# Two small projection matrices moved to the front of two hardware DMA queues

## The chip, the cores and the metric

One core of one Trainium2 chip runs the whole program. The metric is the device time of one execution in microseconds (us). A run's profile gives, besides that time, a span from the first to the last instruction, some 2 us shorter. One run of the kernel before (124.2 us) that was slow is left out of the ratios. The sets of runs were made on different chips, so times are compared as ratios to the kernel before, run in the same set.

## The reference, cut to what matters

A linear attention with a sketched feature map, followed by a feed-forward network (FFN) with a ReLU gate. Inputs q, k, v have shape 4 x 4 x 1088 x 32; S1 and S2 are only 8 x 32.

```python
def phi(x):
    a = np.einsum('rd,bhsd->bhsr', S1, x)
    b = np.einsum('rd,bhsd->bhsr', S2, x)
    return np.einsum('bhsi,bhsj->bhsij', a, b).reshape(*x.shape[:-1], r * r)
q_p, k_p = (phi(q), phi(k))
kv = np.einsum('bhsf,bhsd->bhfd', k_p, v)
z = np.sum(k_p, axis=2)
# num = q_p kv, den = q_p z, x = num / den, then per token:
# (relu(x @ w_gate) * (x @ w_val)) @ w_out
```

Nothing can be projected before both S1 and S2 are on the chip.

## The kernel before: the parts that matter

The loads of the first batch are issued at the start from three engines: SP (SyncE) and ACT (ScalarE), which have a hardware queue each, and GpSimd (POOL), which has a software queue. In the profile SP's queue is q1, ACT's q10 and GpSimd's q0.

```python
xall = const.tile([128, 2, D], FP32, name="xall")
for sm, i in ((S1, 0), (S2, 1)):                      # ACT: S1, then S2, 16 KB each on the chip
    nc.scalar.dma_start(out=xall[:, i], in_=sm[None].to_broadcast([16, R, D]))
for i in range(2):
    load_k0(i, nc.sync)                               # SP: the two halves of k, 272 KB each
load_kq(q4, q, 0)                                     # SP: q, 544 KB
# ... cut: masks on GpSimd ...
for g in range(4):
    load_v(0, g)                                      # GpSimd: v in four pieces
for i in range(2):
    load_w(i)                                         # GpSimd: FFN weights
# ... cut: GpSimd builds mkv and an identity, then load_w(2) ...
```

Then comes the chain that this study is about. It is part of the head, the stretch before the first FFN matmul:

- VectorE (DVE) transposes each half of k (`kT`).
- It turns S into `y`, `s1f` and `s_bd`.
- TensorE (PE) projects k with `s_bd` (line 209).
- DVE moves the result to `kab`, transposes q (`qT`), and with GpSimd forms the outer products `kp`.

A small scheduler in Python, run when the program is built, fixes each engine's order from assumed landing times (`LAND`). Each engine's instructions then ran in that order, waiting where a load was late.

## Time and profile before

| | before |
|---|---|
| median (first three runs) | 123.22 us |
| span of the profiled run | 121.5 us |
| first FFN matmul | 24.03 us |
| from there to the end of the span | 97.5 us |

The page divides the span into 40 slices of 3.04 us; a digit is the busy share in tenths. From the page of the kernel before:

```profile
PE   5008996999999998999999999999999999999940
...
DVE  2215999747999998889584769858774799899940
...
DMA  3899945199926030002002000300300120201003
```

PE reads 0 in slices 2 and 3, while the DMA engines read 8 and 9. The DVE timeline of the kernel before says what it waited for (start, duration, line, operation; the bracket gives the idle time ahead and what ended it):

```profile
3.62 0.74 DVE L197 STREAM_TRANSPOSE kT<-k 128x544 f32<-128x544 f32 x1 [1.81 <-DMA k<-in_k_dram]
8.58 0.24 DVE L177 STREAM_TRANSPOSE y<-xall 128x64 f32<-128x64 f32 x1 [4.21 <-DMA xall<-in_S_dram]
...
9.01 0.74 DVE L197 STREAM_TRANSPOSE kT<-k 128x544 f32<-128x544 f32 x1
11.07 0.85 DVE L216 STREAM_TRANSPOSE kab<-ps_a 128x288 f32<-128x288 f32 x2 [1.32 <-PE ps_a L209]
```

The 4.21 us ahead of `y` are the wait for S.

### The profile page before, as it was taken

Reading aid. Unit: us, or ns where it says so; the run is one execution under the profiler, and the core shown is the slowest. Engines: PE = TensorE matmul, PEld = TensorE weight load, DVE = VectorE, ACT = ScalarE, POOL = GpSimd, SP = SyncE. Lnnn points to the kernel's source line nnn. Section 1 sums busy time; section 2 is a strip of 40 time slices with the busy share of each in tenths; the row PEclk is TensorE's granted clock in tenths of the full one; section 3 lists DMA queues with packets and bytes.
Section 4 is the critical chain, followed back from the end, with each engine's and each line's share of the span. In section 5 each row is a group of like instructions: output and inputs, shape, how many; then the busy total and the mean of one; then the engine's idle time right before and its main releaser. Section 6 shows DMA issues by size and latency. Waiting matters only on the chain.

```text
span 121.5 us, 3061 instructions
## 1 busy us (share of the span) xinstructions
PE 106.6 (88%) x1149; PEld 63.8 (52%) x1149; DVE 90.0 (74%) x184; ACT 81.5 (67%) x160; POOL 63.4 (52%) x84
## 2 busy tenths in 40 slices
PE   5008996999999998999999999999999999999940
PEld 4003673534555765445676646666555666766620
DVE  2215999747999998889584769858774799899940
ACT  3100003377368989778799997879998977987730
POOL 7930816984979997329999232797653000000000
PEclk9999999999999999999999999999999999999996
DMA  3899945199926030002002000300300120201003
GB/s 92 242 220 199 109 145 222 4 298 261 360 26 70 5 86 3 5 11 75 0 5 70 16 0 5 86 0 5 89 0 3 42 50 0 64 22 32 17 0 86
DMA packets 7662, 9.20 MB, mean 76 GB/s; under 512 B 2912, under 2 KB 5216, under 8 KB 7648
## 3 DMA queue, kind: packets, MB, share of 16 engines
q1 hardware_dynamic: 3120, 6.56, 16.8%
q0 software_dynamic: 4144, 2.29, 14.4%
q10 hardware_dynamic: 384, 0.16, 0.7%
q8 instruction: 9, 0.15, 0.5%
q14 instruction: 5, 0.04, 0.1%
HBM read 9.08 MB, written 2.23 MB: 93 GB/s over the span
## 4 chain that ended last, share of the span: by engine, by line
PE 67%; DVE 9%; POOL 9%; DMA 6%; ACT 4%; issue 1%; DVEq 1%; ACTq 1%
PE v_ps L594 18%; PE g_ps L583 17%; PE ot_ps L407 16%; DMA xall<-in_S_dram 6%; PE ps_a L209 4%; PE ps_a L366 4%; POOL qp L234 3%; PE ps_a L389 2%; ACT g_sb L588 2%; DVE kp L234 2%; POOL kp L234 2%; PE ps_a L316 2%; DVE ht L611 1%; POOL v L104 1%; PE kv_ps L250 1%
## 5 line engine op out<-in xcount | busy, mean ns | idle before, releaser
L611 DVE TENSOR_TENSOR ht<-g_sb,v_ps 128x512 f16<-128x512 f16 (+1 forms) x98 | 60.6, 647 | 14.4 <-ACT g_sb L588 6.2
L588 ACT ACTIVATE g_sb<-g_ps 128x512 f16<-128x512 f32 (+1 forms) x108 | 59.4, 585 | 13.3 <-PE g_ps L583 10.6
L594 PE MATMUL v_ps<-xT,wv_sb 128*128 128x512 f16 (+1 forms) x108 | 40.2, 372 | 0.0
L407 PE MATMUL ot_ps<-wo_sb,ht 128*128 128x128 f16 x408 | 39.1, 219 | 0.4 <-DVE ht L611 0.4
L407 PEld LDWEIGHTS <-ht 128*128 128x128 f16 x408 | 30.2, 98 | 16.4 <-issue 1.4
L583 PE MATMUL g_ps<-xT,wg_sb 128*128 128x512 f16 (+1 forms) x108 | 38.0, 377 | 0.8 <-ACT g_sb L588 0.7
L234 POOL TENSOR_TENSOR kp<-kab 128x512 f16<-128x512 f32 (+2 forms) x16 | 16.6, 1057 | 7.3 <-DVE kab L216 7.3
L234 POOL TENSOR_TENSOR qp<-a,qab 128x512 f16<-128x512 f32 (+2 forms) x17 | 17.5, 1049 | 0.3
L605 POOL TENSOR_TENSOR ht<-g_sb,v_sb 128x512 f16<-128x512 f16 x10 | 11.6, 1163 | 8.7 <-ACT v_sb L600 8.7
L594 PEld LDWEIGHTS <-wv_sb 128*128 128x128 f16 x108 | 10.6, 98 | 5.6 <-issue 3.7
L366 PE MATMUL ps_a<-ident,qp 128*128 128x128 f16 (+1 forms) x72 | 10.3, 235 | 1.1 <-ACT qptx L374 0.6
L583 PEld LDWEIGHTS <-wg_sb 128*128 128x128 f16 x108 | 10.0, 100 | 1.4 <-issue 0.7
L374 ACT COPY qptx<-ps_a 128x1024 f16<-128x1024 f16 (+1 forms) x10 | 8.9, 892 | 2.2 <-PE ps_a L366 2.2
L366 PEld LDWEIGHTS <-qp 128*128 128x128 f16 (+1 forms) x72 | 6.4, 104 | 7.0 <-issue 2.2
L209 PE MATMUL ps_a<-kT,s_bd 64*32 64x288 f32 x64 | 4.3, 482 | 6.4 <-DVE s_bd L179 6.4
L104 POOL DMA_DIRECT2D v<-in_v_dram x16 | 8.9, 564 | 0.1
L680 PE MATMUL ot_ps<-zeros 128*128 128x128 f16 x45 | 7.9, 308 | 1.1 <-DVE zeros L151 1.1
L250 PEld LDWEIGHTS <-kp 128*128 128x128 f16 (+1 forms) x72 | 5.9, 106 | 4.6 <-issue 3.2
L250 PE MATMUL kv_ps<-v,kp 128*128 128x64 f16 (+1 forms) x72 | 8.1, 207 | 0.0
L334 POOL TENSOR_TENSOR bw<-qab,qw 128x256 f32<-128x256 f32 (+2 forms) x5 | 3.1, 626 | 8.2 <-DVE qw L325 8.2
L197 DVE STREAM_TRANSPOSE kT<-k 128x544 f32<-128x544 f32 x8 | 5.7, 723 | 1.8 <-DMA k<-in_k_dram 1.8
L270 ACT COPY zs<-kv_ps 128x32 f32<-128x32 f32 x4 | 0.7, 182 | 9.1 <-PE kv_ps L264 9.1
(68 smaller groups left out, 84.4 us busy)
## 6 DMA issues: line engine op xcount, KB each, us to landing
q<-in_q_dram SPq DMA_DIRECT2D x4, 544.0 KB, 6.4
out_dram<-o_sb SPq DMA_DIRECT2D x30, 64.0 KB, 1.7
k<-in_k_dram SPq DMA_DIRECT2D x3, 544.0 KB, 4.2
v<-in_v_dram POOLq DMA_DIRECT2D x8, 72.0 KB, 5.2
k<-in_k_dram SPq DMA_DIRECT2D x2, 272.0 KB, 3.0
v<-in_v_dram POOLq DMA_DIRECT2D x8, 64.0 KB, 5.6
wg_sb<-in_moe_w_gate_dram POOLq DMA_DIRECT2D x1, 384.0 KB, 7.4
wv_sb<-in_moe_w_val_dram POOLq DMA_DIRECT2D x1, 384.0 KB, 8.7
```

The costliest lines, as they stand in the source:

```text
L104: nc.gpsimd.dma_start(out=v4[b][32 * g:32 * g + 32, :, 0:n].rearrange("p h c d -> p h (c d)"), in_=x[:, :, CB[g] * D:(CB[g] + n) * D],)
L209: nc.tensor.matmul(st["ps", key][rp][32 * g:32 * g + 32, lo:lo + 32 * n], s_bd[64 * rp:64 * rp + 64].rearrange("p h r x -> p (h r x)"), xt ...
L234: eng.tensor_tensor(out=dst, in0=a[:, :, :, None].to_broadcast([np, n, R, R]), in1=bb[:, :, None, :].to_broadcast([np, n, R, R]), op=ALU.mult)
L250: nc.tensor.matmul(ps[:, p].rearrange("p (h d) -> p h d", h=2), st["kp", b, c][0:np, p * 128:(p + 1) * 128], v4[b][0:np, 2 * p:2 * p + 2, ...
L366: nc.tensor.transpose(st["qpt", key, p0][:, p, c * n:(c + 1) * n], st["qp", key, p0][0:n, c, p * 128:(p + 1) * 128], ident16[0:n, 0:n])
L374: nc.scalar.copy(out=t[:, :, c0 * n:c1 * n], in_=st["qpt", key, p0][:, :, c0 * n:c1 * n])
L407: nc.tensor.matmul(st["ot", i][:, t], st["ht", i][:, j, t * 128:(t + 1) * 128], wo_sb[:, j], start=(j == 0 and t == 0), stop=True, skip_gr ...
L583: nc.tensor.matmul(st["g", n][:, :cs], wg_sb[:, j], xT[:, c0:c0 + cs], start=True, stop=True)
L588: nc.scalar.activation(out=st["gs", n][:, :cs], in_=st["g", n][:, :cs], func=ACTF.Relu)
L594: nc.tensor.matmul(st["v", n][:, :cs], wv_sb[:, j], xT[:, c0:c0 + cs], start=True, stop=True)
L605: nc.gpsimd.tensor_tensor(out=st["ht", i][:, j, :cs], in0=st["gs", n][:, :cs], in1=st["vs", n][:, :cs], op=ALU.mult)
L611: nc.vector.tensor_tensor(out=st["ht", i][:, j, :cs], in0=st["gs", n][:, :cs], in1=st["v", n][:, :cs], op=ALU.mult)
```

## The change

The intent is to give S1 and S2 a hardware queue's first place each, so that both land early, and to let k follow.

```diff
-LAND = {"s": 4.2, "k": (3.9, 4.9), "q": 6.9, "v": 8.2, "w": (10.8, 13.2, 15.8)}
+LAND = {"s": 3.4, "k": (4.0, 5.0), "q": 7.0, "v": 8.2, "w": (10.8, 13.2, 15.8)}
@@
-    for sm, i in ((S1, 0), (S2, 1)):
-        nc.scalar.dma_start(out=xall[:, i], in_=sm[None].to_broadcast([16, R, D]))
+    for sm, i, eng in ((S1, 0, nc.sync), (S2, 1, nc.scalar)):
+        eng.dma_start(out=xall[:, i], in_=sm[None].to_broadcast([16, R, D]))
     for i in range(2):
         load_k0(i, nc.sync)
     load_kq(q4, q, 0)
```

The new `LAND` moves `y`, `s1f` and `s_bd` ahead of the first k transpose on DVE. PE's and GpSimd's orders stay as they were.

## The prediction

> **What bounds the kernel now.** I began with the page's digits per slice. From about 25 us to 117 us TensorE (PE) reads 9 in nearly every slice, so that stretch is full of work that the change does not touch. Slices 2 and 3 (3 to 9 us) read 0 for PE, nearly 0 for VectorE (DVE): the head of the kernel waits for data. The last releasing chain says for what. This is its start, in order of time (start, duration, what):
>
> ```profile
> 0.81 0.64 ACTq L111
> 1.45 0.03 issue
> 1.48 7.00 DMA xall<-in_S_dram
> ...
> 8.58 0.24 DVE y L177
> 8.82 0.17 DVE s1f L185
> 9.00 0.11 DVE s_bd L179
> ...
> 9.15 1.94 PE ps_a L209 x16
> 11.09 0.83 DVE kab L216 x2
> ```
>
> The reader is to see that the second of two 16 KB transfers, S2, is the longest piece of the head: issued at 1.48, landed at 8.48. Everything up to there hangs on it. I then asked for the transfers of that tile, for time from issue to landing:
>
> ```profile
> DMA to landing us min/median/max: 3.0/5.0/7.0
> ```
>
> Two transfers, so S1 took 3.0 us (0.81 to 3.8) and S2 took 7.0, though both are equal in size and came from the same queue 0.64 us apart. The packets that left on that queue (q10) in the stretches 3:4, 4:5, 5:6, 6:7 and 7:8 us tell why (packets, MB, share of 16 engines):
>
> ```profile
> q10 hardware_dynamic: 118, 0.01, 9.7%
> ...
> q10 hardware_dynamic: 63, 0.01, 8.1%
> ...
> q10 hardware_dynamic: 40, 0.00, 3.3%
> ...
> q10 hardware_dynamic: 25, 0.00, 1.9%
> ...
> q10 hardware_dynamic: 8, 0.00, 0.6%
> ```
>
> S1 was out before 4 us in one burst. S2's 128 small packets dribble out from 4 to 8.4 us, beside q (queue q1) and v and the weights (queue q0). Last, the timeline of DVE and the waits: what stood ready meanwhile?
>
> ```profile
> POOL kp L234 <- DVE kab L216: 4.9, 1, 4.9
> DVE y L177 <- DMA xall<-in_S_dram: 4.2, 1, 4.2
> DVE kT L197 <- DMA k<-in_k_dram: 1.8, 1, 1.8
> ```
>
> k had landed in time: its first half released DVE at 3.62, and the second half took 3.1 us from its issue (transfers of that tile, by window), so it was there by 4.4 us; but its transpose stands behind y, s1f and s_bd in DVE's order and ran at 9.01. From 11.07 on DVE runs without a gap to 15.9 and nearly so to 21.5, and the first FFN matmul starts at 24.03. So the head is a chain: S2, s_bd, k projection, kab, qT, then DVE work.
>
> **What the Trainium skill says.** "DMA: Bandwidth & Descriptors", section "Queues, rings and completion order", says each DMA engine takes turns between the queues that have work, a packet at a time. That agrees with the dribble above: a 128 B packet of S2 waits its turn behind q's and v's large ones, S1 met only k. The same page, "Issuing engines are not separate DMA queues", says that issuing from several engines saves only issue time; so I credit the change with being early, not with a second queue's bandwidth. "SBUF — State Buffer", section "Terms", says DVE and GpSimd lock a shared port pair; the kp products on DVE agree: 845 ns at most while POOL works, 378 ns at least when it doesn't. "TensorE: Matmul & The Clock Gate", Part 1, says that the array runs at half clock until it has been busy for a window of about 3.4 us; the trace agrees, as the same 512-column matmul takes on the chain
>
> ```profile
> 24.21 0.43 PE g_ps L583
> ...
> 28.92 0.22 PE g_ps L583
> ```
>
> **The change part by part.** The comparison of instruction orders says that PE and GpSimd keep theirs; ACT loses one issue, SP gains one; on DVE y, s1f and s_bd move ahead of the first k transpose. So nothing is added or removed, and it is a matter of when four loads land.
>
> S1 goes first on SP (issue 0.81), S2 first on ACT (0.81, not 1.48). The best row for both is S1 of before, first on its queue: 3.0 us. They land at 3.8; I allow 4.0. In the trace y, s1f and s_bd end 0.63 us after the landing (8.48 to 9.11), so s_bd is ready at 4.6, 4.5 us earlier.
>
> k's halves and q move back by one S issue, 0.64 us. The first half: 1.45 plus 2.8 (before) is 4.25; the second: 1.87 plus 3.1 is 5.0. But before, they were out just when v's first packets came (q0 begins shortly before 4 us); now some share turns with v. My estimate adds 0.3 and 0.8: 4.6 and 5.8. A k transpose takes 0.74, so the second ends at 6.5 instead of 9.75. From that end to kab took 1.32 (9.75 to 11.07), so kab starts near 7.85 instead of 11.07, and 0.77 later, at 8.6, DVE could take qT: 3.2 us earlier.
>
> q: issued at 1.73 it took 7.0 us, landing at 8.7, hidden behind S2 until now. Issued at 2.37 the same 7.0 would give 9.4; as S2 no longer takes turns and v's queue is the same I take 9.0. That is after 8.6: **q takes the place of S2 as the wait**, for some 0.4 us. qT then starts at 9.0 instead of 11.84: 2.8 us.
>
> Behind it the DVE work is the same, less a little: POOL's four kp start right at kab (8.8), DVE's three kp later than kab plus qT, so they overlap POOL for some 1.2 us instead of 1.65 (13.10 to 14.75). An overlapped kp costs about twice a lone one, so about 0.2 us is saved. Sum of the head: 2.8 + 0.2 = 3.0 us.
>
> The loads that follow are released by DVE steps (k for the next batch at 15.56), so they move along; these now meet the tail of the output weights, which lands at 6.02 + 9.2 = 15.2. Next batch's k has slack: issued 15.56, 4.0 us to landing, 19.6, used at 21.52. v (lands at 9.6 at the latest, used at 16.6) and the FFN weights (11.2 and 13.1, used at 24.03) have slack of several us too. So the FFN should start about 3.0 us earlier, at 21.0, and the rest is the same order of work. I take off 0.1 for the clock: PE turned fast 3 to 4 us after the FFN began, about the least possible wait, so a shifted start can only meet the window's edge worse. 123.22 - 2.9 = **120.3 us**.
>
> **The rivals.** (1) The gain is full, 3.6 us or more: k and q land as before relative to issue. For it: S2's packets are gone from the crowd, and moves of 0.64 us are small. It would make 119.5. Against it: q's 7.0 us already shows the crowd. (2) q, not S2, is the real bound: if it lands at 10 or later, because its large packets now share all turns with v and weights, gain shrinks to 1.8 us, 121.4. For it: it is last in SP's queue and pushed back further. Against: the turns that S2 took cost it little, as does a shift of 0.64. (3) The head's gain is given back in the FFN's first third, where the chain runs over GpSimd (v loads and qp, 35 to 46 us), or by a later clock window: 1 us of extra half clock costs at most 0.5 us. All of that work is released by what is shifted, so I give it little: 120.8 to 121. (4) S2 stays late, since being on ACT it starts after k anyway. S1 in just that place took 3.0 us, so hardly.
>
> **Range and chances.** The head's sum lies between 2.0 (q late) and 3.7 (nothing new in the way); loss behind it 0 to 0.6. That gives 119.3 to 121.6. Over 2% faster means below 120.8, a gain of 2.4: my middle is 0.5 beyond it, with a spread of about 0.8, so 0.72. Within 2%: 0.27. Slower needs a new wait of over 5 us, for which nothing speaks: 0.01.
>
> **What would show it.** Both S transfers at about 3 us from issue to landing, y at about 4 us; kab near 7.9; a DVE wait for q of some tenths before qT near 9.0; the first FFN matmul near 21.0; from there an equal span to the end (97.5 us before). Wrong if q lands beyond 10, if k's second half lands beyond 6.5, or if the FFN part is longer than before by over 0.6.

## The result

The changed kernel takes 121.41 us (median of four runs, 121.28 to 121.71), against 123.35 us (123.2 to 123.6) before. The ratio is 0.9844, with a 95% interval of 0.9815 to 0.9872. The change is a clear gain of 1.6%, short of 2%.

The start of the chain that ended last, in the changed kernel (start, duration, what; SPq is SP's sequencer issuing, L111 an S load, L99 a k load):

```profile
0.74 0.06 issue
0.80 0.69 SPq L111
1.49 0.06 issue
1.55 0.80 SPq L99
2.35 0.05 issue
2.40 4.55 DMA k<-in_k_dram
...
6.97 0.76 DVE kT L197
...
7.77 1.29 PE ps_a L209 x12
9.06 0.83 DVE kab L216 x2
9.89 1.25 DVE qT L197 x2
```

The long piece is no longer S2 (7.00 us) but the second half of k (4.55 us, landing at 6.95). DVE's timeline of the changed kernel shows the same from the other side:

```profile
3.32 0.24 DVE L177 STREAM_TRANSPOSE y<-xall 128x64 f32<-128x64 f32 x1 [1.51 <-DMA xall<-in_S_dram]
...
5.68 0.75 DVE L197 STREAM_TRANSPOSE kT<-k 128x544 f32<-128x544 f32 x1 [1.83 <-DMA k<-in_k_dram]
6.97 0.74 DVE L197 STREAM_TRANSPOSE kT<-k 128x544 f32<-128x544 f32 x1 [0.55 <-DMA k<-in_k_dram]
9.04 0.85 DVE L216 STREAM_TRANSPOSE kab<-ps_a 128x288 f32<-128x288 f32 x2 [1.32 <-PE ps_a L209]
9.81 1.33 DVE L197 STREAM_TRANSPOSE qT<-q 128x544 f32<-128x544 f32 x2
```

`y` starts 5.26 us earlier, but `kab` only 2.03 us earlier: the new wait is for k. `qT` has no bracket, so q had landed. The first FFN matmul is shifted by the same 2.03 us. From the PE timeline of the changed kernel:

```profile
22.00 0.61 PE L583 MATMUL g_ps<-xT,wg_sb 128*128 128x512 f16 x1
```

From that first FFN matmul to the end of the span are 97.5 us, as before (119.5 - 22.00 against 121.5 - 24.03). So nothing was lost later; what is missing of the forecast gain was lost inside the head.

### The profile page after: what moved, and what is told of

It reads as the page before. It is cut to its first block, busy times and chain, and to the rows that moved or that the text cites. A ratio compares the mean times of both kernels' runs of the same rounds, so it can differ in the third digit from the quotient of the medians.

```text
span 119.5 us, 3061 instructions
## 1 busy us (share of the span) xinstructions
PE 107.2 (90%) x1149; PEld 63.8 (53%) x1149; DVE 90.1 (75%) x184; ACT 81.5 (68%) x160; POOL 63.4 (53%) x84
## 4 chain that ended last, share of the span: by engine, by line
PE 68%; DVE 9%; POOL 9%; DMA 4%; ACT 4%; SPq 1%; issue 1%; DVEq 1%
PE v_ps L594 18%; PE g_ps L583 18%; PE ot_ps L407 17%; PE ps_a L366 4%; PE ps_a L209 4%; DMA k<-in_k_dram 4%; POOL qp L234 4%; PE ps_a L389 2%; DVE kp L234 2%; POOL kp L234 2%; PE ps_a L316 2%; ACT g_sb L588 2%; DVE ht L611 1%; POOL v L104 1%; PE kv_ps L250 1%
## 5 line engine op out<-in xcount | busy, mean ns | idle before, releaser
L234 POOL TENSOR_TENSOR kp<-kab 128x512 f16<-128x512 f32 (+2 forms) x16 | 16.6, 1059 | 5.2 <-DVE kab L216 5.2
L209 PE MATMUL ps_a<-kT,s_bd 64*32 64x288 f32 x64 | 4.8, 483 | 3.8 <-DVE kT L197 3.7
L413 ACT ACTIVATE o_sb<-ot_ps 128x512 f32<-128x512 f32 (+1 forms) x9 | 5.2, 576 | 2.4 <-PE ot_ps L407 2.1
```

Source lines behind the costliest of these rows:

```text
L209: nc.tensor.matmul(st["ps", key][rp][32 * g:32 * g + 32, lo:lo + 32 * n], s_bd[64 * rp:64 * rp + 64].rearrange("p h r x -> p (h r x)"), xt ...
L234: eng.tensor_tensor(out=dst, in0=a[:, :, :, None].to_broadcast([np, n, R, R]), in1=bb[:, :, None, :].to_broadcast([np, n, R, R]), op=ALU.mult)
```

## The experiments

The question was why k landed 2.6 us later (6.95 instead of 4.4) when its issue was meant to slip by 0.64. Two theories: **A**, k starts late because S stands ahead of it; **B**, k then shares the DMA engines' turns with v, which before came only when k was nearly done. A second question was why S2 took 7.0 us before. The table lists every run. Landings are of the profiled run, from issue plus time to landing or from the wait that they ended. "kab" and "FFN" are the starts of `kab` and of the first FFN matmul. "S" is the later of S1 and S2. The last column is the ratio to the kernel before with its 95% interval.

| kernel | S | k halves | kab | FFN | median | ratio |
|---|---|---|---|---|---|---|
| before | 8.5 | 3.6, 4.4 | 11.07 | 24.03 | 123.35 | 1 |
| changed | 3.2 | 5.7, 6.95 | 9.04 | 22.00 | 121.41 | 0.984 (0.982 to 0.987) |
| 1 changed, v held back | 3.2 | 5.1, 5.8 | 7.92 | 21.78 | 121.31 | 0.984 (0.978 to 0.990) |
| 2 before, v held back | 6.0 | 3.4, 4.5 | 8.63 | 21.59 | 121.02 | 0.981 (0.975 to 0.987) |
| 3 S1 between k's halves | 4.9 | 3.6, 6.8 | 8.86 | 21.70 | 121.18 | 0.982 (0.975 to 0.988) |
| 4 S2 on GpSimd's queue | 5.2 | 3.7, 4.6 | 8.36 | 21.21 | 120.61 | 0.978 (0.973 to 0.983) |
| 5 new transfers, old order | 3.2 | 5.65, 7.0 | 9.09 | 22.07 | 121.36 | 0.988 (0.981 to 0.994) |
| 6 before, q behind S2 | 7.7 | 3.6, 4.4 | 10.32 | 23.17 | 121.18 | 0.986 (0.979 to 0.993) |
| 7 changed, v 1 us later | 3.2 | 4.8, 5.6 | 7.74 | 21.44 | 120.74 | 0.982 (0.976 to 0.987) |
| 8 before, q behind S2, v 1 us later | 5.3 | 3.5, 4.3 | 7.87 | 20.72 | 119.89 | 0.974 (0.969 to 0.979) |
| 9 before, v 1 us later | 6.7 | 3.6, 4.4 | 9.30 | 22.15 | 121.84 | 0.986 (0.979 to 0.993) |
| 10 changed, again | 3.3 | 5.9, 7.2 | 9.27 | 22.23 | 121.16 | 0.983 (0.979 to 0.987) |
| 11 number 8, again | 6.1 | 3.6, 4.4 | 8.65 | 21.60 | 120.04 | 0.972 (0.967 to 0.977) |

All eleven gave correct results. Runs 1 to 4 share one set of runs of the kernel before, 5 to 8 another, 10 and 11 a third, and 9 has its own. Each row's landings and starts come from one profile, and the heads scatter: the three profiles of the changed transfers (changed, 5, 10) put k's second half at 6.95, 7.0 and 7.2.

### 1. The changed kernel with v held back

A one-column copy on GpSimd that reads k's last column stands ahead of the v issues, so v and the weights wait for k. The mask work moves ahead of it.

```diff
+    mkv = ... ; ident16 = ...          # moved up, unchanged
+    nc.gpsimd.tensor_copy(out=const.tile([128, 1], FP32, name="gate_v"), in_=k4[0][:, NB * D - 1:NB * D])
     for g in range(4):
         load_v(0, g)
     for i in range(2):
         load_w(i)
```

> The changed kernel, with v's transfers (and the weights behind them) held on GpSimd until k's second half has landed, so nothing but S and q shares the DMA engines with k. Theory A (k starts late: S1 stands ahead of it in SP's queue, 0.74 us of issue and about 1.1 us more until the first packet): k's halves still land late, at about 5.5 and 6.3 us against 5.65 and 6.95, kab starts at about 8.4. Theory B (k is slowed by turns with v's packets): k's halves land 2.8 and 3.1 us after issue as in the kernel before, so at about 4.4 and 5.5, kab at about 7.6. The time itself is spoilt by a side effect, since GpSimd's kp products start about 1 us later behind the delayed v issues: 120.5 to 121.6; the verdict is read from the landings.

k's halves landed at 5.1 and 5.8 us, between the two theories. They took 3.6 and 3.4 us from issue: without v, more than the 2.8 and 3.1 of the kernel before, but less than the 4.1 and 4.5 of the changed one. Both theories hold a part. The time did not follow `kab`. From this run's DVE timeline:

```profile
9.95 2.82 DVE L234 TENSOR_TENSOR kp<-kab 128x256 f16<-128x256 f32 x3
```

These three products took 1.93 us in the changed kernel. GpSimd, busy with the delayed issues, started its own `kp` only at 10.48 us, and DVE's second product, overlapping it, took 1.73 us (0.84 in the changed kernel). The expectation had named GpSimd's late products as a side effect; here DVE's three took 0.9 us longer.

### 2. The kernel before with v held back

The same edit on the kernel before.

> The kernel before, with v and the weights held on GpSimd until k's second half has landed. Theory (S2 was late because each of its packets waited a turn behind v's and q's packets): with v gone S2 shares only with q, about 8 turns of some 0.2 us from 4.15, so it lands near 6.0 instead of 8.48 and the head is about 2.4 us shorter, 121 us. Rival (the second transfer on ACT's queue is late whatever else runs): S2 still lands at about 8.5 and the time stays at 123.3.

From the chain of this run:

```profile
1.47 4.56 DMA xall<-in_S_dram
```

S2 landed at 6.03 us, as expected, and not at 8.5. So being second on ACT's queue is not by itself what held S2 until 8.5. Some 2.4 us of its 7.0 were due to v and the weights beside it.

### 3. S1 between the halves of k

```diff
-    for sm, i, eng in ((S1, 0, nc.sync), (S2, 1, nc.scalar)): ...
-    for i in range(2):
-        load_k0(i, nc.sync)
+    ld(1, nc.scalar), load_k0(0, nc.sync)       # ld(i, eng) loads S1 or S2
+    ld(0, nc.sync), load_k0(1, nc.sync)
```

> The changed kernel with S1 between the two halves of k on SP instead of ahead of both; S2 stays first on ACT. Theory A (S1's place ahead of k delays k): the first half lands at 3.6 to 3.9 us as in the kernel before, S1 near 4.3, the second half near 5.5; kab near 7.8 instead of 9.04, about 120.2 us. Rival (the order among them does not matter, the crowd does): the last of the three lands near 7 us as before and the time is 121.4.

The first half of k was back at 3.6 us, so what stood ahead of it did delay it. But the second half still landed late; DVE's timeline:

```profile
6.79 0.74 DVE L197 STREAM_TRANSPOSE kT<-k 128x544 f32<-128x544 f32 x1 [0.64 <-DMA k<-in_k_dram]
```

Issued at 1.98 us, it took 4.8. Theory A expected 5.5 here and was wrong about the size: the last landing hardly moves (6.8 against 6.95), as the rival had it. That v is what the third transfer met is not tested in this run.

### 4. S2 on GpSimd's queue, ahead of v

```diff
+    ld(0, nc.scalar), ld(1, nc.gpsimd)
     for i in range(2):
         load_k0(i, nc.sync)
```

> k first on SP, S1 first on ACT, S2 first on GpSimd's queue ahead of v: nothing in front of k. Theory A: k's halves land at 3.6 and 4.4 to 5.0 us, S1 and S2 by about 4.0; kab near 7.2. Then the forecast's rival comes true: q, issued at 1.73 and landing near 8.7, becomes the wait before qT (8.7 instead of 9.81), and the time is about 120.3 us. If something else holds the head (S2 slow on GpSimd's queue, landing beyond 5), y's wait for S shows it and the time stays near 121.4.

This edit, like the last, is made on the changed kernel. k's halves landed at 3.7 and 4.6 us, with nothing ahead of them and v 1.1 us later (two changes at once, so it doesn't part A from B). But S2 was late. DVE's timeline:

```profile
5.24 0.24 DVE L177 STREAM_TRANSPOSE y<-xall 128x64 f32<-128x64 f32 x1 [2.33 <-DMA xall<-in_S_dram]
```

GpSimd issued it only at 1.34 us, and it took 3.9. So S2 was again what held the head, and q (8.1 us) was not. The time still came to 120.61 us, better than expected for that branch.

### 5. The new transfers with the old order on DVE

```diff
-LAND = {"s": 3.4, "k": (4.0, 5.0), "q": 7.0, ...}
+LAND = {"s": 4.2, "k": (3.9, 4.9), "q": 6.9, ...}
```

> The changed kernel's transfers with the instruction order of the kernel before (the first k transpose ahead of y, s1f and s_bd on DVE). Theory: the end of the head is set by k's second half (landing 6.95 us) and the transpose behind it; S, landed at 3.2, has room, so y, s1f and s_bd fit between the two halves' transposes and kab still starts at about 9.0; 121.4 us. Rival (the new order on DVE is part of the gain): kab about 0.6 us later, 122.0 us.

`kab` starts at 9.09 us and the time is 121.36 us; the ratio's interval (0.981 to 0.994) holds the changed kernel's 0.984. No part of the gain is seen to come from the reordering on DVE: `y`, `s1f` and `s_bd` fit while DVE waits for k's second half.

### 6, 9 and 8. The kernel before: q behind S2, v later, and both

In 6, q goes to ACT's queue behind S2, where by the order of that queue it should no longer take turns with it; its issue also moves from 1.73 to 2.12 us. In 9, only GpSimd's mask work moves ahead of v, which issues v at 2.45 us instead of 1.51. Number 8 does both.

```diff
-    load_kq(q4, q, 0)
+    load_kq(q4, q, 0, nc.scalar)               # 6 and 8
@@
+    mkv = ... ; ident16 = ...                  # 8 and 9: moved up, unchanged
     for g in range(4):
         load_v(0, g)
```

> The kernel before with q issued on ACT's queue behind S1 and S2 instead of on SP's behind k. Theory (S2's packets wait turns behind q's and v's): with q behind S2 in the same queue, S2 shares with k's tail and v only; it lands at 5.2 to 6.2 instead of 8.48, kab near 8.4, about 120.8 us; q lands by about 8.5 and isn't waited for by more than some tenths. Rival (v alone makes S2 late): S2 lands at 7.5 or later, 122.5 us or more.

> The kernel before with only v's issues delayed by about 1 us (GpSimd's mask work first); q stays on SP. It completes the square with q behind S2 alone (S2 landed at 7.7 in the profiled run, against an expectation of 5.2 to 6.2, a miss), and both together (5.25). Theory: each of the two crowds S2 by itself, so either alone leaves it late; here S2 starts near 4.15, shares with q at some 0.2 us a turn and meets v from about 4.8: landing 6.3 to 7.3, y there, kab near 9.4, about 121.6 us. Rival 1 (v is all of it): S2 lands near 5.3 as with both, 120.0 us. Rival 2 (q is all of it): it stays near 8.5, 123.3 us.

> A candidate: the kernel before with nothing large in front of or beside S2: k's halves first on SP, then S1, S2 and q on ACT in this order, and v delayed by about 1.2 us behind GpSimd's mask work. Theory: S2's packets leave between 4.15 and about 4.6 in a burst, landing near 4.9; k's halves at 3.6 and 4.4; s_bd near 5.5, the second k transpose ends near 6.3, kab near 7.6; q lands near 8, so qT may wait some tenths at 8.4; 119.9 us. If S2 still dribbles (beyond 6), 121 us.

Number 6 missed its expectation in the profiled run, where S2 landed at 7.7 us. But its times scatter (122.34 in the profiled run; 120.80, 120.87 and 121.49 in the others), so by time it lies between the theory and the rival. Number 9 gave 6.7 us, as expected. With both, the chain reads

```profile
1.47 3.80 DMA xall<-in_S_dram
```

a landing at 5.3 us and 119.89 us of time. Even so S2 took 3.8 us from issue, against 3.0 for S1, first in the same queue, in the kernel before.

One profile each is thin ground for such a square. In the six profiles of kernels with both S loads on ACT (before, 2, 6, 8, 9, 11) the span is 112.6 to 113.0 us longer than S2's landing. An estimate of S2's landing in a run without a profile is therefore its span less 112.8: for number 6, 6.2, 6.3 and 6.9; for number 9, 7.4, 7.4 and 6.2; for number 8, 5.6, 5.4 and 5.1. So the profile of number 6 fell on the slowest of its runs, and which of 6 and 9 has the later S2 isn't settled. By time each edit alone is worth 1.4%, and both together 2.6 and 2.8% (numbers 8 and 11): the two crowds, q on one side and v with the weights on the other, cost S2 about the same, and within the noise the costs add up.

### 7. The changed kernel with v 1 us later

> The changed kernel with the mask and identity work of GpSimd moved ahead of v's four issues, which delays v by about 1.2 us and changes nothing else. Holding v back wholly gave k's halves at 5.1 and 5.8 us. Theory (about 1.2 us of the second half's delay are turns with v's packets): v's packets now start near 4.3 instead of 3.1, still amid k, so the second half lands at about 6.2 to 6.5 and kab starts near 8.4: 120.8 us. If v's share is not the cause, 6.95, 9.04 and 121.4 stay.

The edit is that of number 9 on the changed kernel. k's second half is again issued at 2.40 us but now takes 3.2 us instead of 4.5, better than expected. So v's early start, with the weights behind it, had cost it 1.3 us. Most of the further gain in `kab` (1.30 us) didn't reach the FFN (0.56 us), and the ratio doesn't tell this run from the changed kernel. The chain shows one reason:

```profile
2.86 6.50 DMA q<-in_q_dram
...
9.39 0.76 DVE qT L197
```

DVE waited 0.80 us for q. This is the wait that the prediction had put into the changed kernel; it showed here because k was no longer the later one.

### 10 and 11. The changed kernel and number 8 side by side

> The changed kernel once more, to stand beside the candidate on one chip: 0.984 of the kernel before, about 121.4 us; in its profile k's second half lands near 7.0 us and kab starts near 9.0, if that is a property of the kernel and not of one run. If k's landing scatters from run to run, it shows here.

> The candidate (S2 with q behind it on ACT, v about 1 us later, k first on SP) on the same chip as the changed kernel: 0.974 of the kernel before, about 119.9 us, so some 1.5 us under the changed kernel; S2 lands near 5.3, kab starts near 7.9. If the gain over the changed kernel was luck of one chip, the two come within 0.5 us.

On one chip, five rounds each: 121.16 us for the changed kernel and 120.04 us for number 8. The late k came back (7.2 us in this profile), so it is no accident of one run. Number 8 beats both kernels, and of all the runs only it is clear of 2% against the kernel before (0.974 and 0.972, with intervals that end at 0.979 and 0.977); its advantage over the changed one is 1.1 us here, less than the 1.5 us expected. S2's landing in it isn't settled: 5.3 us in one profile, 6.1 in the other, and by the estimate above 5.0 to 5.7 in the other runs of number 11.

## Why the prediction was right, and where it was off

The time lies inside the range, and the outline held: S2 leaves the path, the head shortens, the FFN keeps its length. But it came 1.1 us above the middle, only 0.2 us under the range's upper end, and the odds leaned to a gain of over 2%, which the measured 1.6% is not. One of the three signs that the prediction itself had named for being wrong came true: k's second half landed beyond 6.5. That the number still fits is in part luck: the range was wide because q might be late, and a late k happened to cost about as much. The 121.4 us of rival 2 is nearly the measured time, but its cause, a q landing at 10 or later, isn't what happened. The steps:

- **S lands early and makes room: right.** 3.2 us against the 4.0 allowed.
- **k's second half at 5.8 us: the step that failed.** It landed at 6.95. The prediction had it issued at 1.87; it was issued at 2.40, a term of 0.53 us: SP's first k issue, behind S1's, took 0.80 us instead of 0.40, SP came to that issue at 1.55 instead of 1.45, and the prediction had misread the old issue of the second half by 0.04 (it was 1.27, so 1.91 with its own slip of 0.64). It gave 0.8 us for turns shared with v, on the reading that v's first packets come shortly before 4 us; experiment 7 puts v's cost at 1.3. Together these are 1.0 of the 1.15 us by which the landing was missed; the late landing carries `kab` from the forecast 7.85 to 9.04.
- **q takes the place of S2 as the wait: wrong for this kernel.** q landed at 9.2 us, close to the forecast 9.0, but k held DVE until 9.81. Experiment 7, with k freed, shows the wait for q (0.80 us). The forecast of q was sound; it was hidden by the mis-sized k.
- **0.2 us from less overlap of the products: did not come.** It rested on the wait for q. The three products took 1.93 us, against 1.94 before. In experiment 7, with the wait, they took 1.31.
- **0.1 us lost to the clock: did not come.** 97.5 us before and after.

The sum: a forecast gain of 2.9, less 0.8 for `qT` at 9.81 instead of 9.0, less 0.2, plus 0.1, makes 2.0, as the span shows (2.03). The median moved by 1.94. One more sum in the prediction is off: from 123.22, its own bounds (3.7 at most, 2.0 at least, up to 0.6 lost) give 119.5 to 121.8, not 119.3 to 121.6. The result lies in both.

That the delay of k is in part v's turns rests on experiments 1 and 7, which change when v and the weights start (with GpSimd's mask work moved ahead), and nothing of k. The 0.4 us by which k's first half still takes longer in experiment 7 (3.2 against 2.8 from issue) goes with S standing ahead. Whether that is the queue, the making of descriptors or the first reads, no run here tells.

The packets of the two large queues show the collision. From the DMA view of the kernel before, 3:4 us (packets, MB, share of 16 engines):

```profile
q1 hardware_dynamic: 161, 0.29, 78.5%
q0 software_dynamic: 27, 0.02, 16.8%
...
```

and of the changed kernel, 3:4 us and then 4:5 us:

```profile
q0 software_dynamic: 92, 0.05, 64.0%
q1 hardware_dynamic: 16, 0.03, 10.1%
...
q1 hardware_dynamic: 135, 0.26, 76.2%
q0 software_dynamic: 89, 0.04, 34.5%
```

In the microsecond with the most packets of SP's queue, GpSimd's queue (v, with the weights behind it) sent 27 packets beside k before and 89 after. This fits what the Trainium skill says in "DMA: Bandwidth & Descriptors", section "Queues, rings and completion order", of engines that take turns between queues packet by packet. But sharing turns is not all: in the changed kernel v's packets came first. v was issued at 1.51 us in both kernels; its first packets show up between 3.6 and 3.8 us before, and between 2.8 and 3.0 after, so from 3 to 4 us GpSimd's queue sent 92 packets and SP's only 16. In experiment 7 the same microsecond shows 87 packets of SP's queue (0.19 MB) and none of GpSimd's. The prediction had left v where it was in time, and moved only k into it.

## What to carry to other kernels

When several small and large loads are needed at once, ask which packets will meet, and not only which load is issued first: here moving S forward pushed k into the crowd. What helped in these runs (number 8, 119.89 us) was to hold back what has slack (v, needed at 16.6 us) and to put a large transfer behind the small one that it must not slow, in the same queue. After each such move, look up what the next wait would be; here it was k, and behind k it was q.

## What the Trainium skill lacked or had wrong

- "DMA: Bandwidth & Descriptors", section "Issuing engines are not separate DMA queues", calls the time to issue usually small relative to the DMA. Here an S issue held its sequencer for 0.61 to 0.69 us, a k half for 0.40, and a k half behind S1 for 0.80 (0.57 in number 3); S itself landed 2.1 to 3.0 us after issue where it met little else.
- The same section says that issuing from several engines saves only issue time. The choice of queue also decides who takes turns with whom: q behind S2 in one queue instead of beside it went with an S2 at 5.3 or 6.1 us instead of 6.7 where v was held off (experiments 8, 11 and 9; by the estimate above 5.0 to 6.1 against 6.2 to 7.4), though q was also issued 0.39 us later.
- No page gives the latency of a small transfer in a crowd. A 16 KB transfer took 2.1 us from issue to landing at best and 7.0 us beside q, v and weights.
